# One core, attention chained into two expert layers: how the next batch's attention is fed in beside the dense matmuls

## The chip, the cores and the metric

The kernel runs on one core of a Trainium2 chip. A core has a matmul engine (TensorE, PE in the profile; PEld is its weight load), three elementwise engines (VectorE or DVE, ScalarE or ACT, GpSimd or POOL) and queues that start DMA transfers (SP). The metric is the time of one execution in device microseconds. Three runs of the kernel before took 723.27, 725.94 and 726.9 us, median 725.94.

## The reference

Three stages follow each other, all in fp32.

```python
# 1. attention with 32 landmarks per head: B, H, S, D = 4, 8, 576, 64
q_lm, k_lm = means of 18 consecutive rows of q, k
A, Bm, C = sm(q, k_lm), sm(q_lm, k_lm), sm(q_lm, k)      # sm: softmax of scale * a @ b.T
Z = Bm.T / (largest column sum * largest row sum of Bm)
for _ in range(6):
    Z = 2 * Z - Z @ Bm @ Z
x = A @ Z @ C @ v                                        # as 2304 rows of 512
# 2. gated layer: 512 -> 1536 -> 512
xn = x / sqrt(mean(x * x)) * rms_g
x = (silu(xn @ w_gate) * (xn @ w_val)) @ w_out
# 3. one of 8 experts by argmax for the rows whose x @ w_skip > 0: 512 -> 1024 -> 512
out = x;  out[rows] = x + gate_w * (relu(x @ w1[e]) @ w2[e])
```

## The kernel before

**Tiling.** The attention of a batch is factored: instead of x it forms AT, a [4 heads x 32 landmarks, 576 tokens] matrix for each of two groups of four heads, and a small matrix WT of the rest. The products `P = WT x w_gate` and `WT x w_val` (PE rows `P<-wl,WT` and `P<-wr,WT`) then stand in for the weights of stage 2. P lies in three parts P0, P1, P2 of 512 columns each (in the order's rows P_690, P_694 and P_999), one copy for all batches, so a part can be written anew only when the batch that uses it has done with it. `products(b, q)` computes part q of batch b: four weight loads of w_gate and four of w_val, 64 small matmuls, and a split of each result into a high part (a ScalarE cast) and a remainder (a VectorE subtraction).

**Units.** Stage 2 runs in eight units, two halves of 288 tokens for each of four batches (`u = 2 * b + half`). `run_unit` loops over twelve blocks f: `gemm` for the gate (six matmuls `pg`), `hidden_g` (ScalarE tanh, VectorE), `gemm` for the value (six `pv`), `hidden_v` (VectorE, then a ScalarE cast and a GpSimd subtraction into h_t). Block f uses part f // 4 of P. Then come four column blocks of 36 matmuls each with w_out (`o<-h_t,wo`, 144 in a unit). `finish` sends a unit's result out and computes routing logits beside the next unit. `prep(half)` multiplies AT by the reciprocal norm and splits it into ap_t[half], the moving operand of `gemm`.

**Attention of a batch** is a generator, `attention(b)`, which gives control back after each step (`yield`): for each head group loads of k and q, a VectorE transpose (T) and sum (`ln`, one 128x64 from 128x1152 reduction), scores (`pb`, `sq`), softmax, transposes (`cT`), the second scores (`sk`), a GpSimd multiplication, products with v (`pv<-vt`); then for both groups together six iterations for the inverse (`nr`), `pG`, `pw`, `gram` and `sq<-AT,gram` for the norms, `ms`, a square root on ScalarE, and `rb`, which spreads the norms over the partitions into rbs.

**What sets the order.** Generators in the list `side` are advanced one step at each `slot()`, two slots in each block f and six in each column block of the projection, as long as an estimate of the engines' load stays within SLACK of TensorE's. `drain(g)` runs a generator to its end at once. The order in which instructions are written in this way is a priority: a scheduler at build time then lays out each engine's queue, in which an instruction that was written earlier goes first as soon as it is ready. At run time an engine works through its queue in that order. Before the change attention(1) goes into `side` late in unit 0 and is drained when unit 0 has been written, so all of it stands ahead of unit 1. `products(1, 0)` and `products(1, 1)` are added at blocks 4 and 8 of unit 1 and `products(1, 2)` at block 0 of unit 2.

Of the kernel before, what the change touches and what calls it, by code (L numbers as in the profile page):

```python
# [14 lines left out]
B, H, S, D = 4, 8, 576, 64  # L15
# [47 lines left out]
def attention_moe_kernel(  # L63
# [3 lines left out]
    busy = dict.fromkeys("VAGP", 0.0)  # L67
# [9 lines left out]
    def pool(stack, name, bufs=1, **kw):  # L77
        return stack.enter_context(tc.tile_pool(name=name, bufs=bufs, **kw))

    def rsplit(lo_eng, hi, lo, src):  # L80

        A.copy(hi, src)
        lo_eng.tensor_tensor(lo, src, hi.bitcast(F32), ALU.subtract)
# [41 lines left out]
    def atile(name):  # L125
        if fast:
            return st0.tile([128, S], F32, name=name, tag="wa", bufs=6)
        return at.tile([128, S], F32, name=name, tag="wa", bufs=2)
# [580 lines left out]
    def prep(half):  # L709

        ls = slice(16 * half, 16 * half + 16)
        rv = rbs.rearrange("p (j l) -> p l j", l=L)[:, ls]
        for g in range(2):
            a = atile("ap")[:, 0:NH]
            V.tensor_tensor(
                a.rearrange("p (l j) -> p l j", j=J),
                AT[:, g].rearrange("p (j l) -> p l j", l=L)[:, ls], rv, ALU.mult,
            )
            rsplit(V, ap_t[:, half, g, 0], ap_t[:, half, g, 1], a)
# [48 lines left out]
    def convert_w(i):  # L768

        load_raw(i)  # L770
        w = wo_tile(F32)
        from_f64(w, raws[i], wtile("s64"))
        for a in (1, 2):
            load_raw(i + a)
        SP.dma_start(parts_at(w_d[PARTS[i][0]], i), w)
        wparts[PARTS[i]] = w

    def convert_wout(f):
        r = raw64(f)
        SP.dma_start(  # L780
            r.rearrange("p n t -> p (n t)"),
            w_out.bitcast(I32)[128 * f : 128 * f + 128, :],
        )
        ws = x2_tile(F32) if f % 3 == 2 else wtile("wf")
        w = ws[:, 0]
        from_f64(w, r, ws[:, 1])
        wo_t.append(wo_tile(F32R))
        rsplit(V if f % 2 else G, wo_t[f][:, 0], wo_t[f][:, 1], w)

    def load_w(n, q, last=False):  # L790

        ws = []
        for c in range(2):
            if n == "g" or last:
                w = wtile("wl").rearrange("p c n -> p (c n)")
            else:
                w = raw.tile([128, DM, 2], F32, name="wr", bufs=2)
                w = w.rearrange("p c n -> p (c n)")
            w = w.rearrange("p (i n) -> p i n", n=PC)
            f = DM * q + PC * c  # L800
            for g in range(2):
                SP.dma_start(
                    w[64 * g : 64 * g + 64],
                    w_d[n][256 * g : 256 * g + 256, f : f + PC].rearrange(
                        "(i p) n -> p i n", p=64
                    ),
                )
            ws.append(w)
        wparts[n, q] = ws
# [8 lines left out]
    def product0(q, n, g):  # L818

        ps = bank("P")  # L820
        w = wparts.pop((n, g, q))
        for p in range(2):
            PE.matmul(
                ps[64 * p : 64 * p + 64, :], WTs[0][:, g, p],
                w[:, p], start=True, stop=True,
            )
        hi, lo = ptile(n, g, q)
        rsplit(V, hi, lo, ps)

    def product(b, q, n):  # L830

        pss = [bank("P") for g in range(2)]
        ws = wparts.pop((n, q))

        with tc.manual_schedule(engines={nc.tensor.engine}):
            for c in (1, 0):
                for i in range(KC):  # L840
                    for g in (1, 0):
                        gs = slice(64 * g, 64 * g + 64)
                        PE.matmul(
                            pss[g][32 * i : 32 * i + 32, PC * c : PC * c + PC],
                            WTs[b][gs, i], ws[c][gs, i], start=True, stop=True,
                        )
        for g, ps in enumerate(pss):
            hi, lo = ptile(n, g, q)
            rsplit(V, hi, lo, ps)

    def products(b, q):

        if b == 0:
            for n, g in PIECES:
                product0(q, n, g)
                yield
            return
        last = b == B - 1 and q == NQ - 1
        for n in "g" if last else "gv":
            if (n, q) not in wparts:  # L860
                load_w(n, q)
        for n in "gv":
            product(b, q, n)
            if last and n == "g":
                load_w("v", q, last)
                yield
            elif n == "g" and q < NQ - 1:
                load_w(n, q + 1)
            yield
# [155 lines left out]
    def pair_at(lst, i):  # L1025
        return ld(lst, i, E - 1), ld(lst, i + LP, B - 1)
# [148 lines left out]

    side = []

    def slot():

        for n in "VAG":  # L1180
            busy[n] = max(busy[n], busy["P"])
        for g in side[:]:
            if max(busy[n] for n in "VAG") > busy["P"] + SLACK:
                break
            if next(g, "end") == "end":
                side.remove(g)

    def drain(g):
        for _ in g:
            pass  # L1190
        if g in side:
            side.remove(g)
# [3 lines left out]
    def run_unit(u, before):  # L1196

        for f in range(FC):
            before(f)
            h = hidden_g(gemm(u % 2, f, "g"))  # L1200
            slot()
            hidden_v(f, h, gemm(u % 2, f, "v"))
            slot()
        if u == 0:
            drain(conv)
        elif fin:
            drain(fin.pop())
        x2T = x2T_tile(F32)
        for c in range(KC):
            ps = accbank("o")[:, 0:NH]  # L1210
            for f in range(0, FC, 2):
                project(c, ps, (f, f + 1))
                slot()
            evacuate(x2T, c, ps)
        fin.append(finish(u, x2T))
        side.insert(0, fin[0])
# [24 lines left out]
    def ptile_q(q):  # L1241
        P_t.append(pool(ph1, f"P_p{q}").tile([128, 4, 2, DM], F32R, name=f"P{q}"))
# [6 lines left out]
    late_constants()  # L1249
    fast = False  # L1250
    prep(1)
    att = attention(1)
    raw = None

    def conversions():
        for i in range(NC0, 12):
            convert_w(i)
            yield
            if i == 7:
                drain(products(0, 1))  # L1260
                yield
        nonlocal raw
        start1.close()
        raw = pool(pha, "raw", side="right")
        ptile_q(2)
        drain(products(0, 2))
        yield
        side.append(att)
        for f in range(FC):
            convert_wout(f)  # L1270
            yield

    conv = conversions()

    def before(f):
        if f == 4:
            while not any(w[-1] == 2 for w in wparts):
                next(conv)
        if f == 8:
            while not wo_t:  # L1280
                next(conv)

    side.append(conv)
    run_unit(0, before)
    drain(att)
    pr = []

    def add(g):
        pr.append(g)
        side.append(g)  # L1290

    def drain_all(gs):
        while gs:
            drain(gs.pop(0))

    for u in range(1, 2 * B):
        b, half = u // 2, u % 2
        if half == 0:
            prep(1)

        def before(f):
            if half == 0:
                if f == 0:
                    drain_all(pr)
                    add(products(b, 2))
                if f == 5 and b + 1 < B:
                    side.append(att)
                if f == 8:
                    drain_all(pr)
            elif b + 1 < B:  # L1310
                if f == 4:
                    drain(att)
                    prep(0)
                    add(products(b + 1, 0))
                if f == 8:
                    add(products(b + 1, 1))

            if u == 2 * B - 1 and f in (1, 4, 8):
                next(pre)

        if half == 0 and b + 1 < B:
            att = attention(b + 1)
        if u == 2 * B - 2:

            pha.close()
            late = pool(ctx, "late", side="right")
            xs = [late.tile([128, KC, S], F32R, name=f"xs{t}") for t in "hl"]
            make_hroom()
            first = {}
            pre = early(first)  # L1330
        run_unit(u, before)
# [22 lines left out]
    with tc.For_i(0, npairs) as i:  # L1354
        e, b = pair_at(rest[0], i)
# [36 lines left out]
```

## Time and profile before

| | |
|---|---|
| median of three runs | 725.94 us (723.27 to 726.9) |
| profiled execution | 730.47 us, of which the span is 728.7 us |
| TensorE busy | 667.1 us, 92% of the span |
| VectorE, ScalarE, GpSimd busy | 459.2, 295.1, 145.1 us |
| mean granted TensorE clock | 0.952 of full speed |

Unit 0 ends at 156.6 us of the span and unit 1 at 231.4 us, read from where the twelfth block's last `o` matmul ends. A row of a timeline merges equal instructions that follow each other; in brackets stands how long the engine had waited before them and for which tile of which engine. One fp32 matmul of the program is two records in the trace, so its counts can be twice those of the order. A few records are missing.

### The profile page before, as it was taken

What the parts mean: (1) busy time and instruction counts of PE and PEld (TensorE: products, weight loads), DVE (VectorE), ACT (ScalarE), POOL (GpSimd) and SP (SyncE); (2) the same over time, 40 slices, a digit from 0 to 9 for tenths busy, and PEclk for the clock granted to TensorE, in tenths of its full rate; (3) what the DMA queues carried; (4) which work ended last, traced back from release to release, by engine and by line L of the source; (5) the groups of instructions that cost most, each with busy time, mean ns of one, the idle gap of its engine ahead of it and who ended that gap; (6) DMA issues with size and microseconds to landing.
All of it is one profiled execution on the core that took longest, in us unless ns stands there. A gap on an engine that the chain in (4) does not pass through costs nothing. (4 is left out here: it accounts for less than half of the span.)

```text
span 728.7 us, 13382 instructions
## 1 busy us (share of the span) xinstructions
PE 667.1 (92%) x4961; PEld 573.5 (79%) x4961; DVE 459.2 (63%) x1016; ACT 295.1 (41%) x641; POOL 145.1 (20%) x162
## 2 busy tenths in 40 slices
PE   5468799789999899999999999999999999997997
PEld 5257367678877599977898897899889988986985
DVE  5984888978887577886467966261553463352451
ACT  0773887753314431433341344240443243241340
POOL 4000024313200140220040130040362023021120
PEclk8765799899999999999999999999999999998999
DMA  8686464573125842226732107230541375462344
GB/s 284 216 248 227 143 217 152 176 180 100 46 86 117 196 128 75 93 67 149 187 84 66 64 20 157 69 75 1 166 139 62 101 218 173 130 201 95 128 140 156
DMA packets 79435, 97.12 MB, mean 133 GB/s; under 512 B 16016, under 2 KB 58000, under 8 KB 79376
## 3 DMA queue, kind: packets, MB, share of 16 engines
q1 hardware_dynamic: 79376, 96.33, 44.9%
q8 instruction: 37, 0.61, 0.4%
q14 instruction: 22, 0.18, 0.1%
HBM read 76.97 MB, written 19.34 MB: 132 GB/s over the span
## 5 line engine op out<-in xcount | busy, mean ns | idle before, releaser
L58 PE MATMUL o<-h_t,wo 128*128 128x288 f32 x1152 | 169.6, 303 | 9.2 <-ACT wo L58 3.8
L58 PEld LDWEIGHTS o<-h_t,wo 128*128 128x128 f32 x1152 | 157.9, 191 | 19.2 <-issue 6.7
L58 POOL TENSOR_TENSOR h_t<-h,h_t 128x288 fp32r<-128x288 f32 x96 | 82.2, 860 | 399.9 <-ACT h_t L58 363.8
L58 PE MATMUL pg<-ap_t,P 128*128 128x288 f32 x576 | 104.1, 306 | 3.6 <-DVE h L58 1.8
L58 PE MATMUL pv<-ap_t,P 128*128 128x288 f32 x576 | 98.8, 301 | 2.7 <-DVE h L58 2.4
L58 PEld LDWEIGHTS pg<-ap_t,P 128*128 128x128 f32 x576 | 83.2, 189 | 17.6 <-issue 10.3
L58 PEld LDWEIGHTS pv<-ap_t,P 128*128 128x128 f32 x576 | 82.8, 189 | 8.8 <-DVE h L58 4.1
L58 PE MATMUL ph<-xsh,P 128*128 128x288 f32 x384 | 80.5, 303 | 4.5 <-PEq L1354 4.5
L58 PEld LDWEIGHTS ph<-xsh,P 128*128 128x128 f32 x384 | 64.0, 194 | 5.4 <-issue 5.4
L58 DVE SCALAR_TENSOR_TENSOR h<-h,pg 128x288 f32<-128x288 f32 x96 | 42.5, 447 | 26.3 <-ACT h L58 25.2
L58 PE MATMUL ph<-xsl,P 128*128 128x288 f32 x192 | 57.9, 302 | 0.0
L58 ACT ACTIVATE h<-pg 128x288 f32<-128x288 f32 x96 | 38.9, 410 | 42.4 <-PE pg L58 39.1
L58 ACT CAST h_t<-h 128x288 fp32r<-128x288 f32 x96 | 40.8, 430 | 32.6 <-DVE h L58 32.0
L58 PE MATMUL py<-wo,h_t 128*128 128x512 f32 x210 | 51.6, 395 | 0.3 <-DVE h_t L58 0.3
L58 PEld LDWEIGHTS py<-wo,h_t 128*128 128x128 f32 x210 | 39.3, 188 | 10.2 <-issue 0.8
L58 DVE TENSOR_TENSOR h<-h,pv 128x288 f32<-128x288 f32 x96 | 42.4, 446 | 5.9 <-PE pv L58 3.0
L58 DVE STREAM_TRANSPOSE T<-kq 64x576 f32<-64x576 f32 (+1 forms) x40 | 35.6, 889 | 9.0 <-DMA kq<-in_q_dram 4.6
L58 DVE TENSOR_TENSOR P<-P,P 128x512 fp32r<-128x512 f32 x48 | 31.7, 685 | 12.5 <-ACT P L58 12.1
L58 ACT CAST P<-P 128x512 fp32r<-128x512 f32 x48 | 26.3, 588 | 31.8 <-PE P L58 31.6
L58 PEld LDWEIGHTS ph<-xsl,P 128*128 128x128 f32 x192 | 37.4, 195 | 0.1
L58 POOL TENSOR_TENSOR P<-w1r,P 128x512 fp32r<-128x512 f32 x16 | 21.4, 1341 | 66.3 <-ACT P L58 66.3
L58 DVE SCALAR_TENSOR_TENSOR old<-py,mc,old 128x512 f32<-128x512 f32 (+1 forms) x18 | 13.5, 749 | 31.4 <-PE py L58 31.2
(230 smaller groups left out, 967.2 us busy)
## 6 DMA issues: line engine op xcount, KB each, us to landing
wl<-wg_d SPq DMA_DIRECT2D x36, 256.0 KB, 4.7
wr<-wv_d SPq DMA_DIRECT2D x32, 256.0 KB, 4.8
w1r<-in_moe_w_dram SPq DMA_DIRECT2D x32, 256.0 KB, 3.2
wr<-in_moe_w_gate_dram SPq DMA_DIRECT2D x6, 1024.0 KB, 6.6
wr<-in_moe_w_val_dram SPq DMA_DIRECT2D x6, 1024.0 KB, 6.1
wo<-in_moe_w_dram SPq DMA_DIRECT2D x24, 256.0 KB, 5.3
kq<-in_k_dram SPq DMA_DIRECT2D x8, 576.0 KB, 4.3
kq<-in_q_dram SPq DMA_DIRECT2D x8, 576.0 KB, 4.0
```

The costliest lines, as they stand in the source:

```text
L58: return f(*args, **kw)
```

## The change

The next batch's attention, `prep(0)` and the products for parts 0 and 1 become one generator, `follow(b)`. It pauses before each of the two products until `gate[0]` has been raised, at blocks 4 and 8 of the odd unit, when the part has been used for the last time. Attention(1) is no longer drained behind unit 0; instead the load estimates of the three elementwise engines are set to TensorE's. In unit 1 each slot goes round the side list twice (`rush = 2`). Before an even unit, `follow` is drained as a whole. For the later batches `follow` starts at the same place as the attention before (block 5 of the even unit), and the drains of attention and products at blocks 4 and 0 are gone.

```diff
--- before.py
+++ after.py
@@ -1175,11 +1175,15 @@
 
     side = []
 
+    rush = 1
+
     def slot():
 
         for n in "VAG":
             busy[n] = max(busy[n], busy["P"])
-        for g in side[:]:
+        for g in side * rush:
+            if g not in side:
+                continue
             if max(busy[n] for n in "VAG") > busy["P"] + SLACK:
                 break
             if next(g, "end") == "end":
@@ -1249,8 +1253,20 @@
     late_constants()
     fast = False
     prep(1)
-    att = attention(1)
     raw = None
+    gate = [0]
+
+    def follow(b):
+
+        yield from attention(b)
+        for q in range(2):
+            while gate[0] <= q:
+                yield
+            if q == 0:
+                prep(0)
+            yield from products(b, q)
+
+    nxt = follow(1)
 
     def conversions():
         for i in range(NC0, 12):
@@ -1265,7 +1281,7 @@
         ptile_q(2)
         drain(products(0, 2))
         yield
-        side.append(att)
+        side.append(nxt)
         for f in range(FC):
             convert_wout(f)
             yield
@@ -1282,7 +1298,8 @@
 
     side.append(conv)
     run_unit(0, before)
-    drain(att)
+    for n in "VAG":
+        busy[n] = busy["P"]
     pr = []
 
     def add(g):
@@ -1295,31 +1312,28 @@
 
     for u in range(1, 2 * B):
         b, half = u // 2, u % 2
+        rush = 2 if u == 1 else 1
         if half == 0:
+            drain(nxt)
+            gate[0] = 0
             prep(1)
 
         def before(f):
+            nonlocal nxt
             if half == 0:
                 if f == 0:
-                    drain_all(pr)
                     add(products(b, 2))
                 if f == 5 and b + 1 < B:
-                    side.append(att)
+                    nxt = follow(b + 1)
+                    side.append(nxt)
                 if f == 8:
                     drain_all(pr)
-            elif b + 1 < B:
-                if f == 4:
-                    drain(att)
-                    prep(0)
-                    add(products(b + 1, 0))
-                if f == 8:
-                    add(products(b + 1, 1))
+            elif b + 1 < B and f in (4, 8):
+                gate[0] += 1
 
             if u == 2 * B - 1 and f in (1, 4, 8):
                 next(pre)
 
-        if half == 0 and b + 1 < B:
-            att = attention(b + 1)
         if u == 2 * B - 2:
 
             pha.close()
```

On every engine that computes, the queue up to the end of unit 0 stays as it was. The first place is TensorE's queue where unit 0 ends (its 144 `o` matmuls) and unit 1 begins. Before:

```order
L58 MATMUL o<-h_t,wo 128x288 x144
L58 MATMUL pb<-lmk_1404,bdq 128x32 x2
L58 MATMUL sq<-T,bdq 128x288 x4
L58 MATMUL pg<-ap_t,P_690 128x288 x6
L58 MATMUL pv<-ap_t,P_690 128x288 x5
L58 MATMUL cT<-ident,C 96x128 x3
L58 MATMUL pv<-ap_t,P_690 128x288
L58 MATMUL cT<-ident,C 96x128 x3
L58 MATMUL pg<-ap_t,P_690 128x288 x3
L58 MATMUL sk<-T,bdk 128x288 x4
```

After:

```order
L58 MATMUL o<-h_t,wo 128x288 x144
L58 MATMUL pg<-ap_t,P_690 128x288 x6
L58 MATMUL pv<-ap_t,P_690 128x288 x6
L58 MATMUL pg<-ap_t,P_690 128x288 x6
L58 MATMUL pv<-ap_t,P_690 128x288 x6
L58 MATMUL pg<-ap_t,P_690 128x288 x6
L58 MATMUL lp<-x2T,wcat 32x288 x4
L58 MATMUL pv<-ap_t,P_690 128x288 x5
L58 MATMUL lg<-ident_99,h 128x9 x2
L58 MATMUL lg<-ident_99,h 32x9
```

Attention(1)'s first scores (`pb`, `sq`) stood directly behind unit 0; now nine of unit 1's gate and value groups and the finish of unit 0 (`lp`, `lg`, `x2t`) stand ahead of them.

The second place is TensorE's queue at the end of attention(1), from the last `nr` on. Before, with rows left out ahead of `ms` and behind `rb`:

```order
L58 MATMUL nr<-Y,R 128x64 x2
L58 MATMUL o<-h_t,wo 128x288 x6
L58 MATMUL pG<-Y,blk 128x64 x2
L58 MATMUL o<-h_t,wo 128x288 x10
L58 MATMUL pw<-ident,G_1701 128x128
L58 MATMUL o<-h_t,wo 128x288 x3
L58 MATMUL gram<-GT 128x128
...
L58 MATMUL ms<-onesd,sq 128x1 x4
L58 MATMUL ms<-onesd,sq 64x1
L58 MATMUL o<-h_t,wo 128x288 x19
L58 MATMUL rb<-ident,rms 128x128 x4
...
L58 MATMUL pg<-ap_t,P_690 128x288 x3
```

After:

```order
L58 MATMUL o<-h_t,wo 128x288 x17
L58 MATMUL nr<-Y,R 128x64 x2
L58 MATMUL pG<-Y,blk 128x64 x2
L58 MATMUL pw<-ident,G_2014 128x128
L58 MATMUL gram<-GT 128x128 x2
L58 MATMUL P<-wl,WT 32x256
L58 MATMUL sq<-AT,gram 128x288
L58 MATMUL P<-wl,WT 32x256 x8
L58 MATMUL sq<-AT,gram 128x288 x2
L58 MATMUL P<-wl,WT 32x256
L58 MATMUL sq<-AT,gram 128x288
L58 MATMUL P<-wl,WT 32x256 x6
```

Before, with the rows left out, 6 + 10 + 3 + 11 + 1 + 8 + 19 + 19 + 8 = 85 `o` matmuls of unit 1 stand between the last `nr` and unit 2's first `pg`. Now the last 17 `o` of unit 1 stand ahead of that `nr`, and behind it only the attention's own small matmuls and the 64 of `products(1, 0)` follow up to `pg` (which then stands behind `ms`, `P<-wr`, `rb` and the next attention's first `pb` and `sq`).

The third place is VectorE's queue in the same stretch. `ln<-kq` and the `lmk` transposes belong to attention(2), the batch after. Before:

```order
L58 TENSOR_TENSOR gram<-gram,mask 128x128
L58 STREAM_TRANSPOSE lmq_2665<-ln 64x32 x3
L58 TENSOR_TENSOR gram<-gram,mask 128x128
L58 STREAM_TRANSPOSE lmq_2665<-ln 64x32
L58 TENSOR_TENSOR bdq<-lmq_2665,maskj 128x128
L58 TENSOR_TENSOR sq<-sq,AT 128x288 x4
L58 TENSOR_REDUCE ln<-kq 128x64
L58 TENSOR_TENSOR sq<-sq 128x576
L58 TENSOR_TENSOR P_690<-P,P_690 128x512
L58 TENSOR_SCALAR rms<-ms 128x4
```

After:

```order
L58 TENSOR_TENSOR gram<-gram,mask 128x128
L58 TENSOR_REDUCE ln<-kq 128x64
L58 TENSOR_TENSOR gram<-gram,mask 128x128
L58 TENSOR_TENSOR sq<-sq,AT 128x288
L58 STREAM_TRANSPOSE lmk_2867<-ln 64x32 x4
L58 TENSOR_TENSOR sq<-sq,AT 128x288 x3
L58 TENSOR_TENSOR sq<-sq 128x576
L58 TENSOR_TENSOR P_690<-P,P_690 128x512
L58 TENSOR_SCALAR rms<-ms 128x4
L58 TENSOR_SCALAR rms<-ms 64x1
L58 TENSOR_TENSOR P_690<-P,P_690 128x512
L58 RECIPROCAL rms<-rms 128x4
```

The reduction `ln` stood behind the four `sq` multiplications; now it stands between the two `gram` multiplications, and four `lmk` transposes stand between the first and the second `sq`.

## Rows read from the trace of the kernel before

**Rows 1.** The page, part 1: busy time, share of the span and instructions.

```profile
PE 667.1 (92%) x4961; PEld 573.5 (79%) x4961; DVE 459.2 (63%) x1016; ACT 295.1 (41%) x641; POOL 145.1 (20%) x162
```

**Rows 2.** Windows around unit 1: length, PE, PEld, DVE, ACT, POOL busy; clock, DMA.

```profile
156.60:231.40 74.80, 70.20 (x589) 60.41 (x589) 60.57 (x144) 23.51 (x66) 11.99 (x14) 1.00 0.32 89
231.40:258.00 26.60, 23.25 (x269) 15.51 (x268) 16.00 (x33) 12.88 (x32) 3.44 (x4) 1.00 0.79 183
```

**Rows 3.** TensorE timeline, unit 1 and later: start, time, instruction, [idle before].

```profile
184.49 0.53 PE L58 MATMUL cT<-ident,C 128*96 128x128 f32 x3 [0.97 <-ACT C L58]
...
198.11 0.58 PE L58 MATMUL nr<-Y,R 128*128 128x96 f32 x4
...
199.88 0.58 PE L58 MATMUL nr<-Y,R 128*128 128x96 f32 x4
...
268.40 6.55 PE L58 MATMUL o<-h_t,wo 128*128 128x288 f32 x48
```

**Rows 4.** TensorE timeline, end of attention(1) in unit 1.

```profile
207.97 0.63 PE L58 MATMUL nr<-Y,R 128*128 128x64 f32 x4
...
209.28 0.55 PE L58 MATMUL pG<-Y,blk 128*128 128x64 f32 x4
...
211.05 0.28 PE L58 MATMUL pw<-ident,G 128*128 128x128 f32 x1
...
211.69 0.49 PE L58 MATMUL gram<-GT 64*128 64x128 f32 x2
...
214.50 1.42 PE L58 MATMUL sq<-AT,gram 128*128 128x288 f32 x4
...
216.52 1.24 PE L58 MATMUL sq<-AT,gram 128*128 128x288 f32 x4
217.69 1.09 PE L58 MATMUL P<-wl,WT 64*32 64x256 f32 x30
...
221.05 1.26 PE L58 MATMUL ms<-onesd,sq 128*128 128x1 f32 x10 [1.00 <-DVE sq L58]
...
225.07 1.52 PE L58 MATMUL rb<-ident,rms 128*128 128x128 f32 x10
...
231.43 0.56 PE L58 MATMUL pg<-ap_t,P 128*128 128x288 f32 x3
```

**Rows 5.** VectorE timeline, the same stretch.

```profile
214.15 0.63 DVE L58 STREAM_TRANSPOSE lmq<-ln 64x32 f32<-64x32 f32 x3
214.82 0.29 DVE L58 TENSOR_TENSOR gram<-gram,mask 128x128 f32<-128x128 f32 x1
...
217.31 0.94 DVE L58 TENSOR_TENSOR sq<-sq,AT 128x288 f32<-128x288 f32 x2 [0.90 <-PE sq L58]
218.17 2.16 DVE L58 TENSOR_REDUCE ln<-kq 128x64 f32<-128x1152 f32 x1
220.25 0.74 DVE L58 TENSOR_TENSOR sq<-sq 128x576 f32<-128x576 f32 x1
...
227.08 1.47 DVE L58 TENSOR_TENSOR ap<-AT,rbs 128x288 f32<-128x288 f32 x2 [0.84 <-ACT rbs L58]
```

**Rows 6.** ScalarE timeline, the same stretch.

```profile
222.54 0.49 ACT L58 ACTIVATE rms<-rms,eps 128x4 f32<-128x4 f32 x2 [1.31 <-DVE rms L58]
226.62 0.43 ACT L58 COPY rbs<-rb 128x320 f32<-128x320 f32 x1 [3.59 <-PE rb L58]
...
231.19 1.06 ACT L58 CAST P<-P 128x512 fp32r<-128x512 f32 x2
```

**Rows 7.** Windows at the lower clock, columns as in Rows 2.

```profile
132.73:136.14 3.41, 0.83 (x5) 0.56 (x4) 3.41 (x6) 1.84 (x4) 0.80 (x1) 1.00 0.87 311
136.14:139.55 3.41, 2.55 (x10) 2.55 (x11) 3.26 (x6) 2.57 (x5) 0.81 (x1) 0.50 0.81 258
330.70:334.11 3.41, 3.41 (x26) 2.09 (x26) 0.47 (x4) 0.00 (x0) 0.00 (x0) 0.50 0.16 46
```

**Rows 8.** The page, part 6: DMA issues, KB, microseconds to landing.

```profile
wl<-wg_d SPq DMA_DIRECT2D x36, 256.0 KB, 4.7
```

## Prediction

> **What bounds the kernel now.** I read the page first. TensorE is busy 667.1 us [rows 1], 92% of the span, and no other engine comes near that, so a change of order can only win or lose time in which TensorE waits, or runs at the lower clock. Then I read the windows of TensorE around the place that the change touches most, unit 1, whose attention was written whole ahead of it and is now spread through it. From 156.60 to 231.40 us TensorE is busy 70.20 of 74.80 us and so waits 4.6 us; VectorE is busy 60.57 us, which makes it the engine that TensorE waits for there; the clock is full [rows 2]. From 231.40 to 258.00 us the waits are 26.60 - 23.25 = 3.35 us. Last I went along the timelines of the end of attention(1): 23.5 us pass from its last `nr` at 207.97 to unit 2's first `pg` at 231.43 [rows 4], with almost no wait of TensorE. The order says why: 85 `o` matmuls of unit 1 lie in between. At 6.55 us for 48 [rows 3] one takes 0.136 us, so 85 are 11.6 us of dense work that covers a chain of small dependent steps.
>
> **The change, part by part.** The work on every engine is the same before and after; only where it stands differs. Up to the end of unit 0 I count nothing, since the compute queues are equal. In units 3 and 5 the order changes by a few matmuls, the attention's end still lies among `o` matmuls, and units 4 and 6 begin as before; I count nothing there either, and the cover is the same dense work. What is left is unit 1.
>
> *Removed.* The waits between 156.60 and 231.40 us can all go, at most 4.6 us: -4.6. This is the full price, since I count the new ones afresh.
>
> *The end of attention(1) stands bare.* After the change all of unit 1's `o` matmuls are in front of the last `nr`. Unit 2's first `pg` needs ap_t, which needs rbs, which comes from the end of the chain, and TensorE's queue has nothing else to do but the chain's own matmuls and the 64 of `products(1, 0)`. From the start of the last `nr`, in us:
>
> 1. `nr` to `pG` took 209.28 - 207.97 = 1.31 [rows 4]. On VectorE four `lmq` transposes (0.63 for three, [rows 5]) and one small operation now stand ahead of the addition that `pG` needs, of which about half is hidden by `nr`: `pG` at 1.8.
> 2. `pG` to `pw` took 1.77, part of it behind a transposition on VectorE that now stands elsewhere; I take 1.1: `pw` at 2.9. `pw` to `gram` took 0.64 [rows 4]: 3.5.
> 3. The first `gram` multiplication (0.29) can start when its matmul (0.49) is through, at about 4.0. Then comes the `ln` reduction of attention(2), 2.16 [rows 5], and only behind it the second `gram` multiplication: it ends at 6.8, and the second pair of `sq` matmuls (1.24, [rows 4]) ends at 8.1.
> 4. On VectorE the first `sq` multiplication, four `lmk` transposes (as the `lmq`, 0.84), the three others (0.94 for two, [rows 5]) and the sum (0.74) end at about 10.1.
> 5. `ms`, the square root and the reciprocal: `ms` takes 1.26 [rows 4], the root begins 1.5 after the start of `ms` and takes 0.49 [rows 6], then 0.4 for the reciprocal and the way back: `rb` at 12.6.
> 6. From `rb` to the end of the second copy into rbs 227.05 - 225.07 = 2.0 [rows 4, 6]: 14.6.
> 7. Two `ap` multiplications (1.47, [rows 5]) and the casts and subtractions of ap_t behind them, with two casts of P (1.06, [rows 6]) and one subtraction of P in the queues ahead: the first `pg` starts near 16.2, and the flow of `pg` and `pv` near 17.5.
>
> In these 17.5 us TensorE has 0.63 + 0.55 + 0.28 + 0.98 (`gram`) + 2.66 (`sq`) + 2 x 1.09 (`products(1, 0)`) + 1.26 + 1.52 [rows 4] + about 1.0 for attention(2)'s first `pb` and `sq`, together 11.1. So it waits 6.4: +6.4. The low bound is the same chain without the foreign operations on VectorE and ScalarE (2.16, 0.84, 0.84 and about 1.6), a wait of 1.0; the high bound is the whole stretch of before, 23.5 - 11.1 = 12.4. I take the value of the sum, which uses each row of this very chain.
>
> *New waits inside unit 1.* Attention(1) now starts some 11 us later against the dense work and has to get through in what is left of the unit, so three places get tight. The `cT` of the second head group waited 0.97 behind an `ln` reduction [rows 3]; the same reduction stands there again with the same 21 dense matmuls as cover, and now the small operations of the inverse's beginning stand ahead of it too: 1.7. The first `nr` now comes 46 `o` matmuls (6.3 us) and two groups of `pv<-vt` behind `sk`, where VectorE, ScalarE and GpSimd have some ten dependent operations to do: 1.4. From `nr` to `nr` took 199.88 - 198.11 = 1.77 [rows 3], with ten `o` between; now it is eight at first, and transposes and a 2.16 reduction of attention(2) stand between two of them: 1.4 over all. Together +4.5. The low bound is 0.6 and the high one 8, twice the reduction and twice the other two places.
>
> *The clock.* From 132.73 to 136.14 us TensorE was busy 0.83 us, and in the next window the granted clock was 0.50 of full, 1.2 instead of 2.4 GHz; from 330.70 to 334.11 us it was 0.50 as well, though TensorE counted as busy all the time with small matmuls, `rb` and `P<-wr` among them [rows 7]. The bare tail has both, waits and small matmuls. I take one stretch like that of 330.70, 3.41 us at half speed, half of it lost: +1.7. Bounds 0 and twice the stretch at 136.14, 3.4.
>
> The Trainium skill says in TensorE: Matmul & The Clock Gate, section HAM oscillation — how this bites in real kernels, that the clock is lost when matmul bursts are parted by a long unbroken gap. By that rule the tail, whose longest single wait is that for the reduction, would keep its clock, and the sum would be 1.7 lower. The window at 330.70 differs from it: the clock went without any such gap.
>
> *The sum.* -4.6 + 6.4 + 4.5 + 1.7 = +8.0 us. The profiled execution of before took 730.47 us, so one of after would take 738.5. The median of the runs shown lies 4.5 below the profiled execution, 725.94, so I predict 725.94 + 8.0 = 733.9.
>
> **The rivals.** What can be told from no change is 0.5%, 3.6 us.
>
> *The tail costs only what the old waits cost.* If the small waits inside unit 1 stay at 0.6 to 2 and the tail's at 3 to 5, with the clock kept, the sum is -4.6 + 4 + 1.3 = about +0.7, 726.6. For it speaks that unit 1's dense gates now run 11 us without attention beside them; against it that VectorE is busy 81% of the stretch [rows 2] and that the order itself puts the reduction into the chain.
>
> *Faster.* The chain is shorter than TensorE's own work in it. The place is the same, from the last `nr` to the first `pg`; if it takes under about 12 us instead of 17.5, TensorE waits at most 1.0 there, and with 0 elsewhere and a full clock the gain is -4.6 + 1.0 = -3.6 or a little more, 722. Against it: from `ms` to `pg` alone the trace shows 231.43 - 221.05 = 10.4 us [rows 4], though partly behind dense work, and the steps ahead of `ms` add 10.
>
> *Much slower: the weights come late.* The loads for parts 1 and 2 of batch 1 can only be issued when the buffers of `products(1, 0)` are free, and those are now freed in the tail. A load takes 4.7 us to land [rows 8] and four go out for each half of a part. If unit 2's first blocks wait for them in full once or twice, the sum grows by 5 to 9, to 739 to 743. Before, the same loads were bound in the same way behind the same products, and the waits from 231.40 to 258.00 were 3.35 in all, so I give it little.
>
> That the change does not do what it says is in the first rival: the attention does move beside the dense work at its front, and out of it at its end.
>
> **How the numbers follow.** The forecast (+3.6 to about +13) gets 0.62, the first rival 0.18, faster 0.07, late weights 0.13. Faster by over 0.5% is then 0.07, within it 0.18, slower 0.75. The low ends added give -4.6 + 1.0 + 0.6 = -3.0 and the high ones -4.6 + 12.4 + 8 + 3.4 = +19; all ends at once are unlikely, so I go from +1.1 to +17, 727 to 743, which takes most of the late weights in and leaves out faster and half of no change. The forecast's own range is 729.5 to 739.
>
> **What would show it.** Right: behind unit 1's last `o`, TensorE's busy share falls to about two thirds for some 17 us, with waits put down to VectorE's `gram`, `sq`, `rms` and ScalarE's casts, and a window with a clock under 1 in or just behind it; unit 1 itself ends near 156.6 + 70.2 + 2.1 - 11.1 + 4.5 = 222 us (2.1 being the matmuls that now stand ahead of `pg`) and unit 2's first `pg` stands near 239 instead of 231.43. The step on the inner waits is wrong if the last `nr` starts before 219 or after 226. The prediction is wrong if the time from the last `nr` to the first `pg` is under 13 us, or if units 3 and 5, for which I count nothing, move by more than 3.

## The result, and the profile after

The changed kernel took 736.16 us (median of four runs, 734.6 to 736.5), the kernel before 726.42 in the same comparison (723.27 to 729.91). The ratio is 1.0114, 95% interval 1.0077 to 1.0150: slower. The forecast was 733.9, the range 727 to 743. Ratios here are of undisturbed runs only, so one can differ from the quotient of two medians. The profiled execution took 736.21 us, 5.74 more than that of before.

The page, part 1, of the changed kernel, against [rows 1]: TensorE is busy 5.5 us longer with the same 4961 instructions, and its share still reads 92%.

```profile
PE 672.6 (92%) x4961; PEld 575.8 (78%) x4961; DVE 458.0 (62%) x1016; ACT 295.1 (40%) x641; POOL 143.4 (20%) x162
```

Where the time went, from the two traces:

| stretch | before | after | difference |
|---|---|---|---|
| start to the end of unit 0's last `o` | 156.6 | 152.1 | -4.5 |
| from there to unit 2's first `pg` | 74.8 | 83.4 | +8.6 |
| units 2 and 3 | 123.7 | 121.3 | -2.4 |
| units 4 to 7 and stage 3, to the last `py` | 369.1 | 373.2 | +4.1 |

The first line is no effect of the change: its queues are equal, and only the clock differs (mean granted clock 0.81 before and 0.83 after over this stretch). It also says that the profiled executions understate the change: without the front it is +10.2, near the +9.7 of the medians.

The windows of TensorE in the changed kernel: length, then PE, PEld, DVE, ACT and POOL busy (instructions), clock, DMA share, GB/s. The first two answer to [rows 2]; the third is the bare tail, from the last `nr` to unit 2's first `pg`; then the two stretches of the lower clock, each with the one ahead of it.

```profile
152.10:235.46 83.36, 78.40 (x597) 63.80 (x595) 59.05 (x140) 23.62 (x66) 12.04 (x14) 0.91 0.34 93
235.46:258.00 22.54, 21.30 (x234) 14.21 (x235) 14.94 (x32) 11.84 (x29) 3.19 (x4) 0.89 0.79 168
213.40:235.46 22.06, 19.38 (x113) 9.86 (x113) 11.53 (x30) 5.30 (x12) 0.00 (x0) 0.64 0.47 126
213.40:216.36 2.96, 1.56 (x9) 1.15 (x9) 1.38 (x6) 0.31 (x1) 0.00 (x0) 1.00 0.87 242
216.36:223.19 6.83, 6.47 (x29) 2.90 (x28) 4.43 (x10) 0.27 (x1) 0.00 (x0) 0.50 0.26 79
223.19:226.60 3.41, 2.65 (x24) 1.29 (x23) 1.95 (x4) 1.37 (x3) 0.00 (x0) 1.00 0.54 136
226.60:240.26 13.66, 13.49 (x90) 7.53 (x96) 6.79 (x16) 5.09 (x11) 0.00 (x0) 0.50 0.46 116
```

The reader is to subtract: in the first window TensorE waits 83.36 - 78.40 = 4.96 us, hardly more than the 4.6 of before. What grew is its busy time, by 8.2 us, and the clock column says why: 0.91 instead of 1.00. (Eight instructions more lie in the window, the next attention's `pb` and `sq`, busy 1.4 us.) In all, 20.5 us run at 1.2 instead of 2.4 GHz, where before had full clock; 15.7 of them lie in the tail. Ahead of the first fall TensorE was busy 1.56 of 2.96 us, with only short waits, ahead of the second 2.65 of 3.41.

The timeline of TensorE in the tail (start, time, instruction, [idle before]), against [rows 4]:

```profile
210.26 2.51 PE L58 MATMUL o<-h_t,wo 128*128 128x288 f32 x17
213.41 0.63 PE L58 MATMUL nr<-Y,R 128*128 128x64 f32 x4 [0.63 <-DVE Y L58]
214.70 0.63 PE L58 MATMUL pG<-Y,blk 128*128 128x64 f32 x4 [0.67 <-DVE Y L58]
216.06 0.33 PE L58 MATMUL pw<-ident,G 128*128 128x128 f32 x1 [0.72 <-DVE G L58]
216.74 1.11 PE L58 MATMUL gram<-GT 64*128 64x128 f32 x4 [0.35 <-ACT GT L58]
...
221.06 2.27 PE L58 MATMUL sq<-AT,gram 128*128 128x288 f32 x4
...
225.91 1.55 PE L58 MATMUL ms<-onesd,sq 128*128 128x1 f32 x10 [0.76 <-DVE sq L58]
227.39 2.89 PE L58 MATMUL P<-wr,WT 64*32 64x256 f32 x20
230.21 2.69 PE L58 MATMUL rb<-ident,rms 128*128 128x128 f32 x10
...
233.85 0.43 PE L58 MATMUL pb<-lmk,bdq 128*64 128x32 f32 x4
234.08 1.21 PE L58 MATMUL sq<-T,bdq 128*64 128x288 f32 x4
235.46 0.61 PE L58 MATMUL pg<-ap_t,P 128*128 128x288 f32 x1 [0.17 <-ACT ap_t L58]
```

From the last `nr` to the first `pg` 22.05 us pass (16.2 predicted), with waits of only 0.67 + 0.72 + 0.35 + 0.76 + 0.17 = 2.67. `rb` takes 2.69 instead of 1.52 [rows 4], `sq` 2.27 for four instead of 1.24. The tail is nearly full, and most of it ran at half clock.

VectorE in the same stretch, against [rows 5]: the `ln` reduction stands between the two `gram` multiplications, as the prediction's step 3 has it, but the `sq` multiplications behind it now wait for TensorE (1.06). TensorE waits for VectorE's `sq` only ahead of `ms`, 0.76 us, less than the 1.00 of before [rows 4].

```profile
217.57 0.29 DVE L58 TENSOR_TENSOR gram<-gram,mask 128x128 f32<-128x128 f32 x1 [0.56 <-PE gram L58]
217.78 2.09 DVE L58 TENSOR_REDUCE ln<-kq 128x64 f32<-128x1152 f32 x1
219.78 0.29 DVE L58 TENSOR_TENSOR gram<-gram,mask 128x128 f32<-128x128 f32 x1
...
222.43 0.46 DVE L58 TENSOR_TENSOR sq<-sq,AT 128x288 f32<-128x288 f32 x1 [1.06 <-PE sq L58]
```

### The profile page after: what moved, and what is told of

Read it like the earlier page. It is cut to its first block, busy times and chain, and to the rows that moved or that the text cites. A ratio compares the mean times of both kernels' runs of the same rounds, so it can differ in the third digit from the quotient of the medians.

```text
span 734.5 us, 13382 instructions
## 1 busy us (share of the span) xinstructions
PE 672.6 (92%) x4961; PEld 575.8 (78%) x4961; DVE 458.0 (62%) x1016; ACT 295.1 (40%) x641; POOL 143.4 (20%) x162
## 5 line engine op out<-in xcount | busy, mean ns | idle before, releaser
L58 POOL TENSOR_TENSOR h_t<-h,h_t 128x288 fp32r<-128x288 f32 x96 | 80.7, 843 | 392.9 <-ACT h_t L58 376.2
L58 PE MATMUL pg<-ap_t,P 128*128 128x288 f32 x576 | 101.7, 305 | 4.7 <-DVE h L58 2.5
L58 PE MATMUL pv<-ap_t,P 128*128 128x288 f32 x576 | 101.6, 304 | 0.9 <-DVE h L58 0.7
L58 PEld LDWEIGHTS pg<-ap_t,P 128*128 128x128 f32 x576 | 83.1, 190 | 19.2 <-issue 10.8
L58 PEld LDWEIGHTS pv<-ap_t,P 128*128 128x128 f32 x576 | 83.3, 189 | 6.8 <-issue 2.1
```

Source lines behind the costliest of these rows:

```text
L58: return f(*args, **kw)
```

## The experiments

My theory: the end of attention(1), without the 85 `o` matmuls that lay over it, is what costs, and more by the clock than by waits. The rivals: the weights of batch 1's parts come late; the later batches' new code costs; the filler of an experiment helps by the order it makes, not by the clock. In the diffs `+` is the experiment, `-` the kernel named. `rush` is how often a slot goes round the list of generators in unit 1; 2 in the change.

### e1_drain_again: the attention drained ahead of unit 1

```diff
# against the changed kernel
+    att1 = attention(1)
-        yield from attention(b)
+        yield from att1 if b == 1 else attention(b)
-    for n in "VAG":
-        busy[n] = busy["P"]
+    drain(att1)
-        rush = 2 if u == 1 else 1
+        rush = 1
```

> The changed kernel with one part undone: attention(1) is drained behind unit 0 again and the slots of unit 1 go round once; follow(), the gates and the missing drains in the later batches stay. Theory (the loss is the end of attention(1), which stands behind unit 1's last o matmul without dense cover): all of it comes back, 726 us plus or minus 2, the level of the kernel before (0.99 to 1.00 of it). Rival (the loss is in the later batches, whose products now wait for gates and are not drained): nothing comes back, 734 to 737 us.

Measured: 729.92 us (726.01 to 730.65), ratio 1.0036 [1.0008, 1.0063]. 6.2 of the 9.7 us are gone with this one part. It also lets the attention start as early as before, so not all of this need be the cover's. TensorE's timeline shows the cover back:

```profile
215.11 1.32 PE L58 MATMUL o<-h_t,wo 128*128 128x288 f32 x8
217.49 1.43 PE L58 MATMUL ms<-onesd,sq 128*128 128x1 f32 x10 [1.05 <-DVE sq L58]
218.85 1.33 PE L58 MATMUL o<-h_t,wo 128*128 128x288 f32 x4
```

`o` matmuls stand again between `sq`, `ms` and `rb`, and only 6.8 us run at half clock there (`o` takes 1.33 for four behind `ms`). What remains is not in unit 1: from unit 1's first `pg` to unit 2's `o` it takes 107.5 us, before 109.6. It is in units 5 and 6 (below).

### e2_three_steps and e3_one_step: more and fewer steps a slot

```diff
# against the changed kernel: e2
-        rush = 2 if u == 1 else 1
+        rush = 3 if u == 1 else 1
# e3
+        rush = 1 if u == 1 else 1
```

> The changed kernel with three rounds of the side list in a slot of unit 1 instead of two. In the order the last o matmul of unit 1 then stands ahead of ms instead of ahead of the last nr, so that about 10 of the 22 us between the last nr and unit 2's first pg are bare. Theory (bare stretch is the price): about half of the loss comes back, 729 to 732 us. Rival (later batches): 734 to 737 us. Rival (the doubled steps themselves hurt unit 1): slower than 737 us.

> The changed kernel with one round of the side list in a slot of unit 1 instead of two. In the order one more nr iteration (4 nr matmuls instead of 2) stands behind unit 1's last o. Theory (bare stretch is the price): 2 to 4 us more than the changed kernel, 738 to 741 us. Rival (later batches): unchanged, 735 to 737 us.

Measured: e2 733.88 us (732.12 to 739.94), 1.0087 [1.0057, 1.0117]; e3 748.15 us (745.89 to 750.99), 1.0292 [1.0253, 1.0331]. The medians go the expected way in both: the sooner attention(1) ends against the dense work, the better; but e2's interval overlaps that of the changed kernel. The sizes are not as expected. In e2 the chain is covered up to the last `o` before `ms`, and yet little is won. Its profile is of the slowest of its eight executions (739.94 us), so it need not be typical; in it the lower clock sits in what is still bare, 13.7 us from 226.7 us on:

```profile
223.97 0.80 PE L58 MATMUL o<-h_t,wo 128*128 128x288 f32 x4
225.83 1.44 PE L58 MATMUL ms<-onesd,sq 128*128 128x1 f32 x10 [1.06 <-DVE sq L58]
227.21 2.91 PE L58 MATMUL P<-wr,WT 64*32 64x256 f32 x20
230.05 2.69 PE L58 MATMUL rb<-ident,rms 128*128 128x128 f32 x10
...
235.30 0.61 PE L58 MATMUL pg<-ap_t,P 128*128 128x288 f32 x1 [0.17 <-ACT ap_t L58]
```

In e3 unit 1 grows by 2.5 us against the changed kernel (first `pg` to first `pg`, 85.8 against 83.3), as I thought; but unit 2 grows by 5.1 (63.5 against 58.4). Everything behind the tail is late there, TensorE waits 1.48 us for ScalarE's C and 2.88 us for VectorE's P, and the clock drops once more (256.7 to 260.1). None of TensorE's waits there is put down to a load, so this is not the rival of the late weights.

```profile
256.74 1.19 PE L58 MATMUL lp<-x2T,wcat 128*32 128x288 f32 x8 [2.88 <-DVE P L58]
```

In the changed kernel the window up to 258.00 holds 1.24 us of waiting behind the first `pg`, and 0.70 follows ahead of `lg`, which before's window takes in: 1.94, less than the 3.35 of before [rows 2], so there it does not play.

### e4_filled_tail: useless matmuls in the tail

```diff
# against the changed kernel; six places of attention(1), F = (1, 1, 3, 3, 1, 1)
+    def fill(n, w):
+        ps = atbank("fill")[:, 0:NH]
+        for i in range(n):
+            nc.tensor.matmul(ps, w, AT[:, i % 2, 0:NH], start=(i == 0), stop=(i == n - 1))
...
             V.reciprocal(rms[sl], rms[sl])
+        if b == 1:
+            fill(F[2], sqs[0][:, 0:128])
```

> The changed kernel with 10 matmuls of 128x128 by 128x288 in fp32 added, whose result nothing reads: one each behind the last nr, pG, pw and the sq matmuls, three each behind ms and rb of attention(1); each costs TensorE about 0.6 us at full clock, 6 us together. Everything else is computed as before. Theory (of the loss the larger part is the clock, which falls because TensorE has little to do): the clock stays at full in the tail, the time from the last nr to the first pg falls from 22 to about 18 us, and the whole is 732 to 734 us although there is more to do. Rival (the chain's own waits set the tail, the clock only follows): the tail stays at 22 us or grows by what is added, 736 to 742 us.

Measured: 732.81 us (731.29 to 735.52), 1.0072 [1.0038, 1.0106]. More work, and yet 3.35 us less by the medians, with intervals that overlap; the trace is clearer. The windows of the tail (last `nr` to first `pg`) and behind it, and then TensorE's timeline in it:

```profile
213.00:232.21 19.21, 17.17 (x126) 9.90 (x126) 11.49 (x30) 4.71 (x10) 0.00 (x0) 1.00 0.53 145
232.21:265.20 32.99, 30.93 (x318) 24.61 (x313) 22.05 (x56) 18.40 (x47) 8.05 (x11) 1.00 0.67 147
```

```profile
224.16 1.26 PE L59 MATMUL ms<-onesd,sq 128*128 128x1 f32 x10 [0.85 <-DVE sq L59]
225.35 1.72 PE L563 MATMUL fill<-AT,sq 128*128 128x288 f32 x6
227.00 1.05 PE L59 MATMUL P<-wr,WT 64*32 64x256 f32 x18
227.98 1.52 PE L59 MATMUL rb<-ident,rms 128*128 128x128 f32 x10
```

The clock is 1.00 throughout, `rb` takes its 1.52 again, and the tail is 19.21 us instead of 22.05 although the six `fill` rows in it take 6.3 us. Without them TensorE's own work is 17.17 - 6.3 = 10.8 us. The next attention's `pb` and `sq` stand behind the first `pg` here; without their 1.4 us the changed kernel needs 19.38 - 1.4 = 18.0 for the same work. So by this estimate 7.1 us of its tail were the price of the clock. Not all of this can be won, since at full clock TensorE waits for the other engines instead.

### e7_empty_fill and e9_empty_fill_again: the same matmuls, one column each

```diff
# against e4
-        ps = atbank("fill")[:, 0:NH]
+        ps = atbank("fill")[:, 0:1]
-            nc.tensor.matmul(ps, w, AT[:, i % 2, 0:NH], start=(i == 0), stop=(i == n - 1))
+            nc.tensor.matmul(ps, w, AT[:, i % 2, 0:1], start=(i == 0), stop=(i == n - 1))
```

> The kernel of e4 with the same 10 added matmuls at the same places of the program, but of one column instead of 288, so that they take next to no work. A control for e4. Theory (e4 gained because real work held the clock): nothing is gained, 735 to 738 us, and the clock falls in the tail as in the changed kernel. Rival (e4 gained by other buffers and another order around the added instructions): 731 to 734 us as e4.

> The changed kernel with the ten extra matmuls of the filled tail cut to one column each, once more and in more rounds, because the first profile of it came out disturbed. Two theories. Clock: what the filler did was to keep TensorE at work, and ten matmuls of one column are no work, so the stretch of half clock stays in the tail (about 20 us between 216 and 240, as in the changed kernel) and the time stays near the changed kernel's: 1.010 to 1.014 of before, 734 to 738 us. Order: the filler helped because its instructions shift the queue of TensorE (what stands between the chain's steps, and when weights are taken), then the tail shortens here as well, the last nr to the first pg under 20 us, and the time is that of the filled kernel, about 1.007 of before.

Measured: e7 738.59 us (729.12 to 743.6), 1.0084 [1.0040, 1.0128]; e9 733.9 us (730.25 to 745.43), 1.0079 [1.0044, 1.0114]. By the times neither can be told from e4 nor from the changed kernel, so they decide nothing between the two theories. The profile of e9 says something of the tail, but it is of an execution of 736.11 us that stands alone: five others took 730.25 to 731.70 us, less than e4's median, and four 741.35 to 745.43. Its windows at the lower clock, and the ends of the tail on TensorE's timeline:

```profile
216.98:223.81 6.83, 6.83 (x31) 2.93 (x32) 4.51 (x10) 0.00 (x0) 0.00 (x0) 0.51 0.12 30
227.25:230.66 3.41, 3.41 (x29) 2.35 (x28) 0.81 (x3) 1.02 (x3) 0.00 (x0) 0.52 0.65 149
```

```profile
213.00 0.63 PE L59 MATMUL nr<-Y,R 128*128 128x64 f32 x4 [0.63 <-DVE Y L59]
...
235.09 0.40 PE L59 MATMUL pg<-ap_t,P 128*128 128x288 f32 x1 [0.77 <-ACT ap_t L59]
```

With the same number of extra instructions in the same places the clock falls near 217, as in the changed kernel (216.36), and the tail takes 22.09 us, as there (22.05). So in this execution the order of e4's queue did not make the tail short; what the order theory expected, under 20 us, did not come. Against the clock theory's own number, the lower clock lasts 10.2 us here and not about 20, and the tail is as long all the same: the one-column matmuls are not free, their rows take 3.2 us. Whether the clock fell in the tails of the five faster executions too is not shown, and so it stays open whether e4's gain in time needs the work of its fillers.

### e5_batch1_alone, e6_mix and e10_mix_again: parts of the change, put into the kernel before

```diff
# against the changed kernel, e5: later batches by the code of before
+            elif u > 1 and b + 1 < B:
+                if f == 4:
+                    drain(att)
+                    prep(0)
+                    add(products(b + 1, 0))
+                if f == 8:
+                    add(products(b + 1, 1))
# against e5, e6 and e10: attention(1) drained as before, the sequence held in unit 1 without it
-        yield from att
-    for n in "VAG":
-        busy[n] = busy["P"]
+    drain(att)
+    side.append(nxt)
-        rush = 2 if u == 1 else 1
```

> The kernel before with the change made for batch 1 alone: attention(1) is not drained behind unit 0, unit 1's slots go round twice, the products of batch 1 follow behind the attention and wait for the gates; batches 2 and 3 keep the old code. Units 1 and 2 of TensorE's queue are those of the changed kernel. Theory by now (the bare end of attention(1) costs about 7 us, the later batches about 2.6): 732 to 735 us, 2 to 3 us under the changed kernel. Rival (the later batches' part costs nothing and e1's rest is chance): 735.5 to 737 us.

> The kernel before with attention(1) drained as it was, but batch 1's products as one sequence behind it that waits for the gates at blocks 4 and 8; batches 2 and 3 keep the old code. In the order both products of part 0 then stand among unit 1's o matmuls and all of the attention's end does too. Theory (dense cover kept, products early, later batches' cost gone): 724 to 726 us, level with the kernel before or 1 to 2 us under it. Rival (e1's 2.6 us over before came from units 1 and 2 themselves): 728 to 731 us.

> Leaves nothing out: attention(1) drained into unit 1 as before, batch 1's first products as the held sequence in unit 1, the later batches by the old code. The earlier run gave 0.998 [0.995, 1.001] of before. If the gain is real, it comes from two sides: the old waits at unit 1's start are not those of the changed kernel's tail (no bare tail, last nr followed by o), and the later batches have none of the +2.6 us. Expected 0.996 to 1.000, 723 to 727 us. The rival, that the earlier run was the front's clock phase alone: then 1.000 to 1.003, and from unit 0's last o to unit 2's first o it takes as long as before, 111.8 us, within 1 us.

Measured: e5 731.43 us (728.07 to 736.65), 1.0054 [1.0016, 1.0092]; e6 726.69 (723.35 to 729.88), 0.9979 [0.9951, 1.0008]; e10, the same kernel, 727.71 (723.6 to 729.41), 1.0013 [0.9986, 1.0040]. The change at batch 1 alone is slower, and e1, which holds the rest, is slower as well: +0.54% and +0.36%, together 0.9%, against 1.14% for both. The mix is level with before in two comparisons; the 0.2% of the first did not come again.

The profile of e5 has a second measure of the clock's price. Its rows in the tail follow each other as in the changed kernel; here is the window from the last `nr` to the first `pg`:

```profile
213.75:233.92 20.17, 17.12 (x114) 8.85 (x114) 11.66 (x30) 5.30 (x12) 0.00 (x0) 0.73 0.50 138
```

The clock fell for less of it than there (0.73 against 0.64, 11.0 us at half against 15.7), TensorE's busy time is 2.26 us less, and the tail is 1.9 us shorter.

Where the rest lies is told by the lengths of units 5 and 6, from first `pg` to first `pg`, of all the profiles:

| later batches by | kernels | unit 5 | unit 6 |
|---|---|---|---|
| the code of before | before, e5, e6, e10, e11 | 62.3 to 62.4 | 43.3 |
| the changed code | changed, e1 to e4, e7 to e9 | 64.4 to 64.5 | 44.0 to 44.3 |

TensorE at the start of unit 5's `o`, where attention(3) ends, in the changed kernel and then in e10:

```profile
441.95 1.05 PE L58 MATMUL P<-wl,WT 64*32 64x256 f32 x18
443.59 1.26 PE L58 MATMUL ms<-onesd,sq 128*128 128x1 f32 x10 [0.59 <-DVE sq L58]
444.78 0.89 PE L58 MATMUL P<-wl,WT 64*32 64x256 f32 x12
445.60 3.01 PE L58 MATMUL o<-h_t,wo 128*128 128x288 f32 x11
```

```profile
435.52 1.08 PE L58 MATMUL P<-wl,WT 64*32 64x256 f32 x28
436.54 0.67 PE L58 MATMUL pg<-ap_t,P 128*128 128x288 f32 x3
437.04 1.16 PE L58 MATMUL ms<-onesd,sq 128*128 128x1 f32 x10
438.13 1.06 PE L58 MATMUL pv<-ap_t,P 128*128 128x288 f32 x6
```

It is the tail again, in small. The changed order has taken the last `pg` and `pv` from around `ms`; 3.41 us at half clock follow (445.06 to 448.47: 11 `o` take 3.01 us), up to 1.7 of the 2.1 us. All eight profiles with the changed later code have such a stretch, beginning between 440 and 455 us; none of the five others has. That this stretch is the cause there was not tested by itself, and unit 6's 0.8 us was not followed further.

### e8_drain_at_block_1: the attention drained one block into unit 1

```diff
# against the changed kernel
+    att1 = attention(1)
-        yield from attention(b)
+        yield from att1 if b == 1 else attention(b)
+            if u == 1 and f == 1:
+                drain(att1)
```

> The changed kernel, with attention(1) drained at block 1 of unit 1 instead of being spread through the unit (two rounds in a slot stay). In the order its end, up to rb, lies among unit 1's o matmuls, and the finish of unit 0 (x2t) comes late, around the end of unit 1. Theory (cover is what counts): 728 to 731 us, as e1. Rival (any attention that starts later than unit 1 loses): 733 us or more.

Measured: 732.89 us (727.16 to 737.0), 1.0061 [1.0025, 1.0097]. It stands between the changed kernel and e1 and meets neither end: the time came out above what I expected, and its interval overlaps that of e1, so between draining at the start and one block later nothing is shown. Its profile has the chain up to `rb` among `o` matmuls and only 3.4 us at half clock there, and yet TensorE waits 1.19 and 1.24 us ahead of unit 0's late `x2t` and 1.51 ahead of unit 2's first `pg`. So cover of the chain alone does not set the time.

### e11_mix_filled: a way beyond both kernels

```diff
# against e10; fill as in e4
+            fill(2, sqs[0][:, 0:128])       # ahead of the sum of sq
             V.reciprocal(rms[sl], rms[sl])
+            fill(2, sqs[0][:, 0:128])
```

> The same kernel with four extra matmuls (128x128x288, fp32, their results unused) in attention(1): two before the ms step, where TensorE waited 1.04 us for VectorE at 216.48, and two before rb. In the kernel without them 6.8 us ran at half clock from 218.9, about 3.4 us of lost work at the most. Clock theory: the four cost 4 x 0.57 = 2.3 us, of which about 1.0 lies in the wait, and if they hold the clock the time falls by 0 to 2 us against the kernel without them; if they don't hold it, it rises by 1 to 2 us. The rival, that the stretch of half clock costs nothing there because o matmuls and the chain share the time: then it rises by 1 to 2.5 us although the clock is full.

Measured: 726.91 us (724.79 to 729.57), 1.0013 [0.9992, 1.0035], with a span of 723.7 us as e10 has. The window of the place:

```profile
208.00:236.00 28.00, 26.96 (x253) 19.66 (x254) 19.16 (x41) 9.89 (x19) 0.00 (x0) 1.00 0.68 157
```

Here the clock is full, where e10 had 6.8 us at half, and from unit 1's first `pg` to unit 2's first `o` it takes 104.4 us against 107.4. Of these 3.0 us nothing is left at the end: from there to stage 3's first `ph` it takes 294.3 against 291.2, among it a new stretch at half clock at 356 us. So no version that beats the kernel before was found.

## Why the prediction was right, and where its sum was not

**The place: right. What it costs there: in the main not what I said.** The end of attention(1) stood bare behind unit 1's last `o`, and draining it early again (e1) took back 6.2 of 9.7 us. I priced it by waits, and it was paid by the clock. In the clock of before's span (4.5 us added for the front) unit 2's first `pg` stands at 240.0, predicted near 239.

**The term for TensorE's waits in the tail (+6.4): too large.** 2.67 us were measured. The order of VectorE that the step rests on was there, the reduction between the `gram` multiplications included. But TensorE's own work, for which I had 11.1 us, took 19.4. (Without `pb` and `sq` I had 10.1; e4 has 10.8 at full clock.) TensorE was busy 88% of the tail and not two thirds, and behind slow matmuls little time is left to wait in.

**The term for the clock (+1.7): the mis-sized one.** I took one stretch of 3.41 us, as at 330.70 [rows 7]; it was 20.5 us, and the tail's part of the loss is about 7.1 us, estimated from e4. The bound of 3.4 that I gave it was false, too: I put it at two such stretches, though none of my rows shows so long a run of small matmuls with nothing dense among it, and so none could bound it. The stretch at 136.14 alone lasted 6.83 us, to 142.97; my row shows its first half.

**The new waits inside unit 1 (+4.5): too large.** They were 0.74 ahead of `pb`, 0.85 ahead of `cT` and 0.63 ahead of the last `nr`, 2.2 in all; the iterations of `nr` between did not wait. So unit 1's last `nr` stood at 217.9 in the clock of before, ahead of the 219 that I had named as the sign of this step being wrong, and the unit's `o` matmuls ended near 217 and not 222.

**Units 2 to 7 (0): two errors of opposite sign.** Units 2 and 3 were 2.4 us faster, in part because the stretch of [rows 7] at 330.70 is gone (e2, e3 and e9, with the changed code, have one in unit 3 as well, so its absence need not be the change's doing); units 4 to 7 and stage 3 were 4.1 slower, of which 2.9 go with the changed code in units 5 and 6 and 1.1 lie in unit 4, which took 51.0 to 53.7 us in the profiles with the code of before and 52.1 to 53.7 in the others. That the attention's end there "still lies among `o` matmuls" was the wrong sentence: what the traces differ in is `pg` and `pv` around `ms`.

The sum over the tail and unit 1 was +8.0 and came out as +8.6, from waits of 4.96 where I had 10.9 and a clock that cost about four times my figure. That the total fits is in good part luck: two errors of nearly the same size and opposite sign. The two are not independent, since slow matmuls fill time in which TensorE would else wait; that they exchange one for one is not shown, for the tail took 22.05 us in the changed kernel, 20.17 in e5 with less of it at half clock, and 19.21 in e4 with none.

**The rule on the clock.** The Trainium skill, in TensorE: Matmul & The Clock Gate, section HAM oscillation — how this bites in real kernels, ties the loss to long unbroken gaps between bursts. In this tail no wait reaches 0.8 us and the clock was at half for 15.7 of its 22.05 us; the measurement decides, and the window at 330.70 of before had been the better guide.

**The rivals.** "Same" and "faster" fell by the interval. The late weights did not show: from 200 to 272 us TensorE waits for no load in the changed kernel, nor in e3.

## What to carry to other kernels

Before a step is moved, look in the queue order at what dense work stands between the end of its dependent chain and whoever needs it; if none is left, count the chain bare. Do not price such a chain by TensorE's waits alone: read the clock column, and take its small matmuls at half speed as the one case and the waits at full speed as the other, and do not simply add them; this rests on the tail of this kernel alone. A busy share that stays at 92% says nothing here, because slow matmuls count as busy.

## What the runs showed of the hardware

Useless matmuls shortened a dependent stretch: with ten of 288 columns the clock stayed at 2.4 GHz and the tail took 19.21 us; with ten of one column, in the one execution shown, it fell to 1.2 GHz and the tail took 22.09; without any, 22.05. The same rows took 20.17 us where 11.0 us of them ran at half clock (e5) and 22.05 where 15.7 did. And the granted clock can be at half while TensorE counts as busy nearly all the time (13.49 of 13.66 us from 226.60 on) with the small matmuls of a dependent chain and the first `pg` and `pv` behind it.
